# Loading q and k by head pairs, moving casts and rotations between engines, and a reordered front, in an attention-then-MLP kernel

## The chip, the cores and the metric

The kernel runs on one core of one Trainium2 chip. The core has five engines that this text names: TensorE (PE; its weight loads are listed as PEld), VectorE (DVE), ScalarE (ACT), GpSimd (POOL) and SyncE (SP), which here only issues transfers. Sixteen DMA engines move data between DRAM and the on-chip memory SBUF; matrix products land in PSUM. The metric is the device time of one execution in microseconds (us).

## The reference

Banded attention over 8 batches, 8 heads, 576 positions and head width 64, and then a two-layer MLP with an ELU between:

```
scores = q @ k^T / 8                     # per batch and head
scores masked where |row - column| > 32
attn   = exp(scores) / sum(exp(scores))
x      = attn @ v                        # as 4608 tokens x 512
h      = x @ w_in                        # 512 -> 2048
g      = h where h > 0, else exp(h) - 1
out    = g @ w_out                       # 2048 -> 512, float32
```

## The kernel before

**The loop.** The MLP is a loop of 144 steps (`for kk`, L529). A tile of tokens has 256 rows, so there are 18 tiles, and each takes eight steps of two 128-wide groups of the hidden layer. In step kk, TensorE computes `mm1(kk)` (L481, 8 products of 256 columns, L489); ACT takes exp of it (`e_sb`, L495); DVE subtracts 1 (`m_sb`, L497) and, in the next step, takes the ELU (`g_sb`, L502). `mm2` (L508, 4 products of 512 columns, L516) lags two steps behind. At a tile's last step its result is copied out of PSUM by ACT and DVE and written by a transfer of SP (L524 to L526). Up to step 18 `mm1` has two buffers in PSUM, after that three.

**The attention.** Queries are taken in 36 pairs of 64-row blocks, each block against the 128 keys around it. A pair is spread over three steps: `scores` (L277, 32 small products for a pair of blocks counted with both heads of a head pair; then exp on ACT into `pu`, L291), `mask` (DVE, L300), `pv` (L304, products with v and a column of ones, L312), `normalize` (DVE, L321 and L324, into `x_st`), and a transpose of `x_st` into `xT`: by TensorE and a DVE copy for pairs 0 to 7 (`x_transpose` L329, `x_evac` L345), by a transposing transfer on SP's queue from pair 8 on (`x_dma`, L348). Tile t of the MLP needs pairs 2t and 2t+1. Pair i of 8 and more begins at step max(4(i-2)-6, begin of the pair before + 3).

**q and k.** They arrive in float32 (`load_qk`, L107, tile `f`) with 96 partitions, each holding 6 positions of all 8 heads: for one transfer both sides count 96 outermost, then 8 heads, then a run of 768 or 1536 bytes. They are needed transposed, the head width on the partitions, as `qT` and `kT`. For batch 0 they come in halves and are cast to bfloat16 by DVE and ACT (`cast_qk`, L215), transposed on TensorE (`transpose_qk`, L257, 96x96 each, tile `ptx`, L265) and copied out of PSUM. Batch 1 likewise, in halves, at steps 7 to 17. For batches 2 to 4 the casts run on POOL (L463), two to three steps ahead of the transposes (L464), with the copies on ACT. For batches 5 to 7 ACT casts them (`cast_rows`, L236), a transfer on ACT's queue writes them to DRAM (`write_rows`, L247), and a transposing transfer on SP's queue reads them back (`transpose_rows`, L253).

**v and the weights.** They are cast while they are transferred, by POOL's queue (`load_v` L119, `load_w_in` L140, `load_w_out` L147). v lies in `V_e`; a copy moved by 64 rows, `V_o`, is made by two transfers of SP (`rotate_v`, L127). Each weight comes in four chunks; chunk c is needed from step 0, 2, 8 and 12 on.

**What sets the order.** All of it is written out by hand: each engine runs its instructions in the order in which the program emits them, and `at(step, slot, function)` (L404) places attention work in the slots of a step ("dve" after the ELU, "mid" after `mm1`, "end" after `mm2`). An instruction that waits holds up everything behind it on its engine or queue. A `gate` (L135) is a one-element transfer on SP's queue that waits for a weight chunk, and so holds back the loads behind it. Tiles are reused in rings: two buffers each for `f`, three for V.

Of the kernel before, what the change touches and what calls it, by code (L numbers as in the profile page):

```python
# [15 lines left out]
def _bap(ap, new_ap, off=0):  # L16
    return bass.AP(tensor=ap.tensor, offset=ap.offset + off,
                   ap=[list(x) for x in new_ap])
# [3 lines left out]
def kernel(  # L22
# [19 lines left out]
    NQB = S // QB  # L42
    NPAIR = B * NQB // 2
    HP = H // 2
    SJ = 6
    SP_ = S // SJ
    VS = 5
    VD = D + 1

# [36 lines left out]
    def ps_tile(shape, dt, tag, name):  # L86
        return pools[tag].tile(shape, dt, tag=tag, name=name)
# [18 lines left out]

    def load_qk(b, which, part):  # L107
        z, nj = part
        if (b, which) not in qk_f:
            qk_f[b, which] = lpool.tile([SP_, H * SJ * D], FP32,  # L110
                                        tag=f"f{which}", name=f"f{which}")
        t = qk_f[b, which]
        n = H * nj * D
        nc.sync.dma_start(
            out=t[:, z * n:(z + 1) * n].rearrange("p (h x) -> p h x", h=H),
            in_=(q, k)[which][b, :, z * SP_ * nj:(z + 1) * SP_ * nj, :]
            .rearrange("h (p j) d -> p h (j d)", j=nj))

    def load_v(b, m):  # L119
        lo = 128 * m - WIN  # L120
# [5 lines left out]

    def rotate_v(b, m0=0, m1=VS - 1):  # L127
        e, o = V_e[b % 3], V_o[b % 3]
        nc.sync.dma_start(out=o[0:64, m0:m1], in_=e[64:128, m0:m1])
        nc.sync.dma_start(out=o[64:128, m0:m1], in_=e[0:64, m0 + 1:m1 + 1])  # L130

    gate_t = cpool.tile([1, 8], BF16, name="gate_t")
    gates = [0]
# [20 lines left out]
    def w_in_at(c):  # L154
        return w_in_sb[0:1, 0, (c + 1) * (D_FF // 4) - 1:(c + 1) * (D_FF // 4)]

    for i in range(3):
        nc.vector.memset(V_e[i][:, :, :, D:VD], 1.0)
        nc.vector.memset(V_e[i][0:32, 0], 0.0)
        nc.vector.memset(V_e[i][96:128, VS - 1], 0.0)  # L160
        if i < 2:
            for c0, n in ((KPAD - WIN, HP), (KPAD + HP * S, 1)):
                z = kT[i][:, c0:c0 + WIN]
                nc.vector.memset(_bap(z, [z.ap[0], [S, n], [1, WIN]]), 0.0)
# [4 lines left out]
    for part in (HALF_A, HALF_B):  # L169
        for which in range(2):  # L170
            load_qk(0, which, part)
    for m in (1, 2, 0, 3, 4):
        load_v(0, m)
    rotate_v(0, 0, 2)
    rotate_v(0, 2, VS - 1)
    load_w_in(0)


# [30 lines left out]
    def copy_on(eng, d_, s_):  # L209
        if eng is nc.scalar:  # L210
            nc.scalar.copy(d_, s_)  # L211
        else:
            eng.tensor_copy(d_, s_)  # L213

    def cast_qk(b, which, part, hps, eng):  # L215
        z, nj = part
        hp0, nh = hps[0], 2 * len(hps)
        n = H * nj * D
        s_ = qk_f[b, which][:, z * n + 2 * hp0 * nj * D:
                            z * n + (2 * hp0 + nh) * nj * D]  # L220
        s_ = _bap(s_, [s_.ap[0], [nj * D, nh], [D, nj], [1, D]])
        t = lpool.tile([SP_, nj, nh * D], BF16, tag=f"b{which}", name="qkb",
                       bufs=4)
        qk_b[b, which, z, hp0] = t
        copy_on(eng, _bap(t, [t.ap[0], [D, nh], [nh * D, nj], [1, D]]), s_)

    def keys_or_queries(b, which):
        if which == 0:
            return qT[b % 2]
        return kT[b % 2][:, KPAD:KPAD + HP * S].rearrange(  # L230
            "p (g s) -> p g s", g=HP)


    rows, in_dram = {}, {}

    def cast_rows(b, which, hp):  # L236
        if hp == 0:
            rows[b, which] = lpool.tile([SP_, SJ, H * D], BF16,
                                        tag=f"r{which}", name="rows", bufs=1)
        n = SJ * D  # L240
        s_ = qk_f[b, which][:, 2 * hp * n:(2 * hp + 2) * n]
        d_ = rows[b, which][:, :, 2 * hp * D:(2 * hp + 2) * D]
        nc.scalar.copy(  # L243
            _bap(d_, [d_.ap[0], [D, 2], [H * D, SJ], [1, D]]),
            _bap(s_, [s_.ap[0], [n, 2], [D, SJ], [1, D]]))

    def write_rows(b, which):  # L247
        t = dpool.tile([S, H * D], BF16, tag=f"d{which}", name="in_dram")
        in_dram[b, which] = t
        nc.scalar.dma_start(  # L250
            out=t.rearrange("(p j) c -> p j c", j=SJ), in_=rows.pop((b, which)))

    def transpose_rows(b, which):  # L253
        nc.sync.dma_start_transpose(
            out=keys_or_queries(b, which), in_=in_dram.pop((b, which)))

    def transpose_qk(b, which, part, hps, evac, tag="t0"):  # L257
        z, nj = part
        src = qk_b.pop((b, which, z, hps[0]))
        nh = len(hps)  # L260
        W = 512 if nh > 1 else 1024
        pt = ps_tile([128, nh, W], BF16, tag, "ptx")
        for g in range(nh):
            for j in range(nj):
                nc.tensor.transpose(  # L265
                    pt[:, g, j * SP_:(j + 1) * SP_],
                    src[:, j, g * 128:(g + 1) * 128], ident[0:SP_, 0:SP_])
        n = SP_ * nj
        d = keys_or_queries(b, which)[:, hps[0]:hps[0] + nh, z * n:(z + 1) * n]
        pitch = d.ap[1][0] if nh > 1 else n  # L270
        copy_on(evac,
                _bap(d, [d.ap[0], [pitch, nh], [nj, SP_], [1, nj]]),
                _bap(pt, [pt.ap[0], [W, nh], [1, SP_], [SP_, nj]]))

    st = {}

# [65 lines left out]
            xT[t] = xpool.tile([128, 2, NDO, 128], BF16, tag="xT", name="xT")  # L342
        return xT[t][:, z, :, :]

    def x_evac(i):  # L345
        nc.vector.tensor_copy(xT_of(i), st.pop(i))  # L346

    def x_dma(i):  # L348
        x_st = st.pop(i)[3]
# [4 lines left out]
        return NQB * b // 2  # L354


    warm = cpool.tile([128, 1], FP32)
    nc.vector.memset(warm, 0.0)
    nc.scalar.activation(warm, warm, AX.Exp)

    def front_qk(part, tags):
        for g in range(2):
            hps = (2 * g, 2 * g + 1)
            cast_qk(0, 0, part, hps, nc.vector)
            cast_qk(0, 1, part, hps, nc.scalar)
            transpose_qk(0, 0, part, hps, nc.scalar, tags[g])
            transpose_qk(0, 1, part, hps, nc.vector, tags[2 + g])

    front_qk(HALF_A, ("h0", "h1", "y0", "y1"))
    for i, tag in ((0, "s"), (1, "u")):  # L370
        scores(i, tag)
    for i in (0, 1):
        mask(i)
    front_qk(HALF_B, ("h0", "h1", "y0", "y1"))
    for fn in (pv, normalize, x_transpose, x_evac):
        for i in (0, 1):
            fn(i)

    gate(w_out_sb[0:1, NFO // 4 - 1, D_MODEL - 1:D_MODEL])
    for which in range(2):  # L380
# [3 lines left out]
    for c in range(2, 4):  # L384
        load_w_in(c)
        load_w_out(c)
    rotate_v(1, 0, 2)
    gate(w_in_at(3))
    for which in range(2):
        load_qk(1, which, HALF_B)  # L390
    for m in range(3, VS):
        load_v(1, m)
    rotate_v(1, 2, VS - 1)
    for which in range(2):
        load_qk(2, which, WHOLE)
    for m in range(VS):
# [7 lines left out]
    def at(kk, slot, fn, *args):  # L404
        tasks.setdefault((kk, slot), []).append((fn, args))
# [14 lines left out]
    for i, tag in ((2, "s"), (3, "u")):  # L420
        at(0, "mid", scores, i, tag)
        at(1, "dve", mask, i)
        at(1, "mid", pv, i)
        at(2, "dve", normalize, i)
        at(2, "mid", x_transpose, i)
        at(3, "dve", x_evac, i)
    at(4, "dve", swap_pools)

    allh = tuple(range(HP))
    for part, kq in ((HALF_A, 8), (HALF_B, 16)):  # L430
        for which in range(2):
            at(kq - 1, "mid", cast_qk, 1, which, part, allh,
               (nc.scalar, nc.vector)[which])
            at(kq + which, "mid", transpose_qk, 1, which, part, allh,
               nc.scalar, "s")
    pair_at(4, 10)
    pair_at(5, 13)
    pair_at(6, 18)
    pair_at(7, 21)

# [2 lines left out]
    for i in range(8, NPAIR):  # L443
        kk = begin[i] = max(HALF * (i - 2) - 6, begin[i - 1] + 3)
        at(kk, "mid", scores, i)
        at(kk + 1, "dve", mask, i)
        at(kk + 1, "end", pv, i)
        at(kk + 2, "dve", normalize, i)
        at(kk + 2, "end", x_dma, i)
    for b in range(2, B):  # L450
        k0 = begin[first_pair(b)]
        if b >= 3:
            kk = max(k0 - 26 if b < 5 else k0 - 36, 18)
            at(kk, "mid", load_qk, b, 0, WHOLE)
            at(kk + 1, "mid", load_qk, b, 1, WHOLE)
            for m in range(VS):
                at(kk + 2 + m // 3, "mid", load_v, b, m)
        if b < 5:
            for n in range(2 * HP):
                which, hp = n // HP, n % HP  # L460
                kk = k0 - (8 if b == 2 else 10) + n
                at(kk - 2 - b // 3, "mid", cast_qk, b, which, WHOLE, (hp,),
                   nc.gpsimd)  # L463
                at(kk, "mid", transpose_qk, b, which, WHOLE, (hp,), nc.scalar)  # L464
        else:
            for which in range(2):
                c0 = k0 - 27 + 8 * which
                for hp in range(HP):
                    at(c0 + (0, 1, 4, 5)[hp], "end", cast_rows, b, which, hp)
                at(c0 + 6, "mid", write_rows, b, which)  # L470
                at(c0 + 9, "mid", transpose_rows, b, which)
        at(k0 - HALF, "mid", rotate_v, b)

# [94 lines left out]
```

The softmax here doesn't subtract the row's maximum and nothing guards it: scores larger than these inputs give would overflow.

## Time and profile before

The median of 13 runs is 337.62 us (335.95 to 343.52). The profiled execution took 337.12 us in all, of which its span, first instruction to last, is 335.3; 1.8 us lie around it. Its granted TensorE clock was 0.998.

| | |
|---|---|
| first `mm1` begins | 26.46 us |
| step 16, 32, 48, 97, 143 begins | 64.34, 104.75, 140.82, 239.21, 326.56 us |
| last product ends, span ends | 330.5, 335.3 us |
| q and k of batch 0, second half of k landed | 14.91 us |
| first chunk of w_in, second of w_out landed | 19.84, 30.46 us |
| ACT, cast of 96x768 (`rows`) | 820 ns |
| ACT, copy of 128x512 (`y_sb`); exp 128x1024 (`pu`) | 587, 1018 ns |
| ACT, copy of a transposed 128x576, 128x1152 | 633, 1118 ns |
| DVE, cast of 96x1536; copy of 128x512 bfloat16 out of PSUM | 944, 415 ns |
| DVE, ELU; minus 1 (medians) | 692, 427 ns |

Steps are counted in the timeline by the groups of eight products of L489. In the profile's rows, "out<-in" names the tiles, xN the count, "<-" after a bracket what ended the idle time before an instruction; a queue's engine is written with a q (SPq). The windows view gives, for each stretch, its length and then each engine's busy time with the number of its instructions.

### The profile page before, as it was taken

The page shows a single profiled execution, that of the slowest core. Times are in us where ns is not written, and L with a number is a line of the kernel's source. Part 1 is how long each engine was busy: PE and PEld are TensorE (multiplying, and loading weights), DVE is VectorE, ACT ScalarE, POOL GpSimd, SP SyncE. Part 2 cuts the span into 40 slices and gives each one's busy share as a digit, 9 for nine tenths or more (in the row PEclk, how much of TensorE's full clock was granted, in tenths as well). Part 3 has the DMA queues.
Part 4 walks back from the last instruction along what each step waited for, and adds up shares of the span by engine and source line. Part 5 has one row for each costly group of instructions (what it writes and reads, how often), then busy time and mean ns, then how long its engine had stood idle before and what let it go on. Part 6 is the DMA issues. An engine that isn't in the chain of part 4 may idle for free.

```text
span 335.3 us, 7736 instructions
## 1 busy us (share of the span) xinstructions
PE 303.3 (90%) x3152; PEld 201.5 (60%) x3152; DVE 240.3 (72%) x446; ACT 171.5 (51%) x262; POOL 63.4 (19%) x84
## 2 busy tenths in 40 slices
PE   0347999798899998899999999999999999999994
PEld 0235666565666665576666666666666666666661
DVE  4456767687686779676778777687878777877662
ACT  1624265565556634488655566566644443443431
POOL 8442320086461119100111100000000000000000
PEclk9999999999999999999999999999999999999999
DMA  8999999999999999948999999979492320202011
GB/s 174 186 229 206 212 182 190 216 287 228 127 154 170 231 203 185 165 91 168 184 233 221 172 259 199 229 138 251 83 158 74 86 80 18 78 18 81 0 63 63
DMA packets 93862, 52.72 MB, mean 157 GB/s; under 512 B 67908, under 2 KB 87364, under 8 KB 93828
## 3 DMA queue, kind: packets, MB, share of 16 engines
q1 hardware_dynamic: 51428, 39.79, 56.4%
q0 software_dynamic: 41728, 8.92, 39.2%
q10 hardware_dynamic: 672, 3.54, 3.3%
q8 instruction: 24, 0.39, 0.5%
q14 instruction: 10, 0.08, 0.1%
HBM read 36.70 MB, written 12.98 MB: 148 GB/s over the span
## 4 chain that ended last, share of the span: by engine, by line
PE 80%; DMA 7%; DVE 6%; ACT 3%; issue 2%; SPq 0%; DVEq 0%
PE ps L489 36%; PE psY L516 34%; DMA xT<-x_st 4%; PE psS L312 3%; PE psS L284 3%; PE ptx L265 3%; DMA f<-in_k_dram 2%; DMA Vo<-Ve 2%; DVE m_sb L497 1%; DVE g_sb L502 1%; ACT e_sb L495 1%; DVE x_st L324 1%; ACT pu L291 1%; ACT qkb L211 1%; DVE xT L346 1%
## 5 line engine op out<-in xcount | busy, mean ns | idle before, releaser
L495 ACT ACTIVATE e_sb<-ps 128x512 f32<-128x512 f32 x144 | 86.0, 597 | 144.1 <-PE ps L489 142.0
L489 PE MATMUL ps<-xT,w_in_sb 128*128 128x256 bf16 x1152 | 150.8, 274 | 5.1 <-DVE xT L346 3.3
L516 PE MATMUL psY<-w_out_sb,g_sb 128*128 128x512 bf16 x576 | 148.1, 379 | 0.3 <-DVE g_sb L502 0.2
L489 PEld LDWEIGHTS <-w_in_sb 128*128 128x128 bf16 x1152 | 110.4, 98 | 42.4 <-issue 5.0
L502 DVE SCALAR_TENSOR_TENSOR g_sb<-ps,m_sb 128x512 bf16<-128x512 f32 x144 | 99.4, 690 | 13.8 <-DVE m_sb L497 0.5
L497 DVE TENSOR_SCALAR m_sb<-e_sb 128x512 bf16<-128x512 f32 x144 | 67.4, 468 | 57.9 <-ACT e_sb L495 56.4
L516 PEld LDWEIGHTS <-g_sb 128*128 128x128 bf16 x576 | 52.6, 98 | 38.6 <-DVE g_sb L502 0.7
L123 POOL DMA_DIRECT2D Ve<-in_v_dram x40 | 34.1, 858 | 95.7 <-PE psS L312 81.3
L291 ACT ACTIVATE pu<-psS 128x1024 bf16<-128x1024 f32 x36 | 36.5, 1019 | 1.8 <-PE psS L284 1.6
L265 PE MATMUL ptx<-ident,qkb 96*128 96x96 bf16 x240 | 17.6, 221 | 14.8 <-DVE qkb L213 12.3
L324 DVE TENSOR_TENSOR x_st<-psS,rc 128x512 bf16<-128x512 f32 x36 | 24.9, 692 | 3.4 <-DMA xT<-x_st 2.3
L300 DVE TENSOR_TENSOR pm<-pu,masks 128x1024 bf16<-128x1024 bf16 x36 | 25.2, 701 | 2.2 <-ACT pu L291 2.0
L213 POOL CAST qkb<-f 96x768 bf16<-96x768 f32 x24 | 20.8, 904 | 29.3 <-DMA f<-in_q_dram 23.6
L265 PEld LDWEIGHTS <-qkb 96*128 96x128 bf16 x240 | 14.3, 105 | 16.7 <-DVE qkb L213 12.9
L312 PEld LDWEIGHTS <-pm 128*64 128x64 bf16 x576 | 12.5, 113 | 17.3 <-DVE pm L300 12.0
L243 ACT CAST rows<-f 96x768 bf16<-96x768 f32 x24 | 19.7, 822 | 0.0
L312 PE MATMUL psS<-Ve,pm 128*64 128x65 bf16 x320 | 16.5, 200 | 0.5 <-DVE pm L300 0.3
L284 PE MATMUL psS<-qT,kT 64*128 64x64 bf16 x576 | 15.3, 196 | 1.6 <-DVE xT L346 0.9
L312 PE MATMUL psS<-Vo,pm 128*64 128x65 bf16 x256 | 14.5, 200 | 2.4 <-DMA Vo<-Ve 1.6
L284 PEld LDWEIGHTS <-kT 64*128 64x128 bf16 x576 | 11.2, 98 | 9.0 <-issue 7.6
L211 ACT COPY qT<-ptx 128x576 bf16<-128x576 bf16 (+1 forms) x18 | 12.4, 689 | 4.4 <-PE ptx L265 4.4
L525 DVE COPY y_sb<-psY 128x512 f32<-128x512 f32 x18 | 12.3, 685 | 2.0 <-PE psY L516 2.0
(29 smaller groups left out, 64.6 us busy)
## 6 DMA issues: line engine op xcount, KB each, us to landing
out_dram<-y_sb SPq DMA_DIRECT2D x18, 512.0 KB, 3.3
f<-in_q_dram SPq DMA_DIRECT2D x6, 1152.0 KB, 12.4
f<-in_k_dram SPq DMA_DIRECT2D x6, 1152.0 KB, 15.3
in_dram<-rows ACTq DMA_DIRECT2D x6, 576.0 KB, 3.8
Vo<-Ve SPq DMA_DIRECT2D x12, 260.0 KB, 5.0
Ve<-in_v_dram POOLq DMA_DIRECT2D x24, 128.0 KB, 13.1
f<-in_q_dram SPq DMA_DIRECT2D x4, 576.0 KB, 9.7
f<-in_k_dram SPq DMA_DIRECT2D x4, 576.0 KB, 12.0
```

The lines of the kernel that those rows point to most:

```text
L123: nc.gpsimd.dma_start(out=V_e[b % 3][p0:p1, m, :, 0:D], in_=v[b, :, lo + p0:lo + p1, :].rearrange("h p d -> p h d"))
L265: nc.tensor.transpose(pt[:, g, j * SP_:(j + 1) * SP_], src[:, j, g * 128:(g + 1) * 128], ident[0:SP_, 0:SP_])
L284: nc.tensor.matmul(psS[:, h % 2, hp * 128 + z * QB:hp * 128 + (z + 1) * QB], lhsT=kT[b % 2][base:base + 64, KPAD + hp * S + QB * qb - WIN: ...
L291: nc.scalar.activation(pu, _bap(psS, [psS.ap[0], [1, 1024]]), AX.Exp, scale=SCALE)
L300: nc.vector.tensor_mul(pm, pu, _bap(mm, [mm.ap[0], [0, H], [1, 2 * QB]]))
L312: nc.tensor.matmul(psS[QB * z:QB * (z + 1), par, hp * VD:(hp + 1) * VD], lhsT=pm[:, par * HP + hp, z * QB:(z + 1) * QB], rhs=vv[:, qb // 2 ...
L324: nc.vector.tensor_mul(x_st, _bap(psS, [psS.ap[0], [VD, HP], [512, 2], [1, D]]), _bap(rc, [rc.ap[0], [2, HP], [1, 2], [0, D]]))
L489: nc.tensor.matmul(ps[:, j, :], lhsT=w_in_sb[:, do, fo * 128:(fo + 1) * 128], rhs=xT[t][:, :, do, :], start=(do == 0), stop=(do == NDO - 1))
L495: nc.scalar.activation(e_sb, ps, AX.Exp)
L497: nc.vector.tensor_scalar(m_sb, e_sb, -1.0, None, ALU.add)
L502: nc.vector.scalar_tensor_tensor(g_sb, psH.pop(kk), 0.0, m_t.pop(kk), ALU.max, ALU.min)
L516: nc.tensor.matmul(psY[t][ts], lhsT=g_sb[:, j, ts * 128:(ts + 1) * 128], rhs=w_out_sb[:, s * FG + j, :], start=(s == 0 and j == 0), stop=( ...
```

## The change

- q and k are loaded with 128 partitions: a partition holds 18 positions (9 in the halves) of two heads, four head pairs by 32 runs of positions. Each load is two transfers, one for each head of the pairs. The source of a transfer counts 4 outermost, then 32, then a run of 2304 or 4608 bytes; the destination counts 128, then that run.
- Casts go by positions, 768 columns each for whole batches, and all are on ACT or DVE, none on POOL. Transposes on TensorE are 128x128: 18 for each of q and k of a batch, where it was 24 of 96x96.
- Batches 3 to 7 go through DRAM (before: 5 to 7). Batch 2 is cast by ACT from step 17 on and transposed on TensorE in steps 19 to 26. Batches 3 to 7 are loaded 30 steps ahead of their first pair (batch 3 at step 18) and cast from 18 steps ahead on.
- `rotate_v` is two DVE copies of 64 partitions, 2080 columns for a whole batch, where it was two transfers.
- In the front, casts and transposes are regrouped (q, then k, each in pieces of 5 and 4 positions), copies of `xT` go to ACT, and `idle(n)` puts n products of zeros, 512 columns each, into TensorE's order at six places.
- Pairs 4 and 5 begin one step earlier (9 and 12).

```diff
     def load_qk(b, which, part):
         z, nj = part
-        n = H * nj * D
-        nc.sync.dma_start(
-            out=t[:, z * n:(z + 1) * n].rearrange("p (h x) -> p h x", h=H),
-            in_=(q, k)[which][b, :, z * SP_ * nj:(z + 1) * SP_ * nj, :]
-            .rearrange("h (p j) d -> p h (j d)", j=nj))
+        t = lpool.tile([128, 2, nj * D], FP32, tag=f"f{which}{nj}",
+                       name=f"f{which}")
+        qk_f[b, which, z] = t
+        src = (q, k)[which][b, :, z * NC * nj:(z + 1) * NC * nj, :].rearrange(
+            "(g h) (c j) d -> g c h (j d)", h=2, j=nj)
+        for h in range(2):
+            nc.sync.dma_start(out=t[:, h, :], in_=src[:, :, h, :])
...
     def rotate_v(b, m0=0, m1=VS - 1):
         e, o = V_e[b % 3], V_o[b % 3]
-        nc.sync.dma_start(out=o[0:64, m0:m1], in_=e[64:128, m0:m1])
-        nc.sync.dma_start(out=o[64:128, m0:m1], in_=e[0:64, m0 + 1:m1 + 1])
+        nc.vector.tensor_copy(o[0:64, m0:m1], e[64:128, m0:m1])
+        nc.vector.tensor_copy(o[64:128, m0:m1], e[0:64, m0 + 1:m1 + 1])
...
+    def idle(n, tag):
+        ps = ps_tile([128, 512], FP32, tag, "ps_idle")
+        for _ in range(n):
+            nc.tensor.matmul(ps, lhsT=zeros[:, 0:128], rhs=zeros,
+                             start=True, stop=True)
...
+    idle(12, "y1")
+    front_cast(0, HALF_A, nc.vector)
+    front_transpose(0, HALF_A, nc.scalar, ("h0", "h1"))
+    idle(5, "u")
+    front_cast(1, HALF_A, nc.scalar)
+    front_transpose(1, HALF_A, nc.vector, ("y0", "y1"))
     for i, tag in ((0, "s"), (1, "u")):
         scores(i, tag)
+    idle(8, "h1")
+    front_cast(0, HALF_B, nc.vector)
+    front_transpose(0, HALF_B, nc.scalar, ("h0", "h1"))
     for i in (0, 1):
         mask(i)
-    front_qk(HALF_B, ("h0", "h1", "y0", "y1"))
-    for fn in (pv, normalize, x_transpose, x_evac):
-        for i in (0, 1):
-            fn(i)
+    front_cast(1, HALF_B, nc.scalar)
+    idle(4, "y1")
+    front_transpose(1, HALF_B, nc.scalar, ("y0", "y1"))
+    rotate_v(0, 0, 2)
+    idle(4, "h1")
+    for i in (0, 1):
+        pv(i)
+    for i in (0, 1):
+        normalize(i)
+    rotate_v(0, 2, VS - 1)
+    idle(4, "h1")
+    for i in (0, 1):
+        x_transpose(i)
+    for i in (0, 1):
+        x_evac(i, nc.scalar)
...
-    pair_at(4, 10)
-    pair_at(5, 13)
+    at(10, "dve", rotate_v, 1, 0, 2)
+    at(17, "dve", rotate_v, 1, 2, VS - 1)
+    pair_at(4, 9)
+    pair_at(5, 12)
...
+    starts = set(begin.values()) | {9, 12, 18}
+    LEAD = 18
     for b in range(2, B):
         k0 = begin[first_pair(b)]
         if b >= 3:
-            kk = max(k0 - 26 if b < 5 else k0 - 36, 18)
+            kk = max(k0 - 30, 18)
             at(kk, "mid", load_qk, b, 0, WHOLE)
             at(kk + 1, "mid", load_qk, b, 1, WHOLE)
...
+        groups = [(which, j0) for which in range(2) for j0 in (0, 6, 12)]
+        if b == 2:
+            free = [f for f in range(17, k0) if f not in starts]
+            for n, (which, j0) in enumerate(groups):
+                at(free[max(n - 1, 0)], "end", cast_qk, b, which, WHOLE, j0,
+                   6, nc.scalar)
+                at(free[n + 1], "mid", transpose_qk, b, which, WHOLE, j0,
+                   6, nc.scalar)
         else:
-            for which in range(2):
-                c0 = k0 - 27 + 8 * which
-                for hp in range(HP):
-                    at(c0 + (0, 1, 4, 5)[hp], "end", cast_rows, b, which, hp)
-                at(c0 + 6, "mid", write_rows, b, which)
-                at(c0 + 9, "mid", transpose_rows, b, which)
-        at(k0 - HALF, "mid", rotate_v, b)
+            free = [f for f in range(k0 - LEAD, k0) if f not in starts]
+            for n, (which, j0) in enumerate(groups):
+                at(free[n], "end", cast_qk, b, which, WHOLE, j0, 6, nc.scalar)
+                if j0 == 12:
+                    at(free[n], "end", write_rows, b, which)
+                    at(free[n] + 4, "mid", transpose_rows, b, which)
+        at(k0 - HALF - 1, "dve", rotate_v, b)
```

The first pair of batches 2 to 7 begins at step 27, 39, 58, 74, 94 and 110 in both kernels.

## The prediction

> **What bounds the kernel now.** I read the page's shares and rows over time first, then the windows by stage, the timeline at the start of the loop, the queues' table, the waits, and last the loads' tile `f`.
>
> ```profile
> PE 303.3 (90%) x3152; PEld 201.5 (60%) x3152; DVE 240.3 (72%) x446; ACT 171.5 (51%) x262; POOL 63.4 (19%) x84
> ...
> PE   0347999798899998899999999999999999999994
> ...
> DMA  8999999999999999948999999979492320202011
> ...
> q1 hardware_dynamic: 51428, 39.79, 56.4%
> ...
> q10 hardware_dynamic: 672, 3.54, 3.3%
> ...
> f<-in_q_dram SPq DMA_DIRECT2D x6, 1152.0 KB, 12.4
> f<-in_k_dram SPq DMA_DIRECT2D x6, 1152.0 KB, 15.3
> ```
>
> TensorE is full but for the first tenth; the DMA engines are full for two thirds of the span. The windows (length, then PE, PEld, DVE, ACT, POOL with counts, clock, DMA share, GB/s):
>
> ```profile
> 0.00:27.00 27.00, 8.93 (x123) 6.88 (x124) 12.72 (x30) 8.88 (x12) 15.14 (x28) 1.00 1.41 198
> ...
> 50.00:130.00 80.00, 74.65 (x873) 50.05 (x871) 60.23 (x106) 44.35 (x69) 30.08 (x36) 1.00 1.40 198
> 130.00:235.00 105.00, 103.21 (x1079) 68.01 (x1077) 79.58 (x149) 65.04 (x101) 11.58 (x14) 1.00 1.15 193
> ```
>
> To 27 us TensorE waits for q and k; then it is the bound. The loop, 26.46 to 330.5, is 304.0 us. A plain step takes 1.735 us (steps 133 and 134 begin at 309.20 and 310.94): 144 x 1.735 = 249.8. Steps 100 to 104, with one pair of attention, take 7.88 us against 4 x 1.735 = 6.94, so a pair costs 0.94: 34 pairs in the loop, 32.0. Transposes of q and k: 24 groups of six at 0.26 and 4 of twelve at 0.51, 8.2; of x, 1.3. That makes 291.3. The other 12.7 us are waits (9.1 from step 3 on, the largest 2.02 at 64.34 and 1.1 at 86.53 and 140.82) and a slow start:
>
> ```profile
> 26.46 1.87 PE L489 MATMUL ps<-xT,w_in_sb 128*128 128x256 bf16 x8 [0.52 <-DVE xT L346]
> ...
> 29.23 1.41 PE L489 MATMUL ps<-xT,w_in_sb 128*128 128x256 bf16 x8
> ```
>
> The same eight products take 0.87 later on.
>
> **The loads, the part that decides.** Now `f`'s source counts 96 outermost, and so does its destination. After the change the source counts 4 outermost (head pairs), then 32, and the destination 128. How many of the 16 DMA engines a transfer uses follows its shape: queue 1's packet records hold 2018 completion packets of 4 bytes, which are 16 for each of the 58 plain transfers (their outermost counts are 64, 96 or 128), 32 for each of the 34 transposing ones, and 1 for each of the two gates, which move one element. Both plain cases fit the largest number up to 16 that divides the outermost counts of both sides. For 4 and 128 that is four engines. No transfer of this trace has such a shape; its ends are sixteen, as for all loads so far, and one, as for a gate. I leave out one, since 4 and 128 share more than a gate's count of 1 does, and take four.
>
> The Trainium skill ("DMA: Bandwidth & Descriptors", sections "Why a DMA increments its semaphore by 16 and not by 1" and "Rules for kernel authors") states the same rule and warns that an outermost count under 16 confines the whole transfer to that many engines; no run here shows a count of 4. By that page the sum is the four-engine one below; by the row of the other loads, the sixteen-engine one.
>
> With four engines: q and k are 16 tensors of 1.18 MB, 18.87 MB, so 4.72 MB for each engine. What one engine moves in 1 us: 13.4 KB in the loads of now (1536 bytes in 115 ns), 14.8 in V_o's copies (4160 bytes in 281 ns), 20.1 in queue 10's writes (6144 bytes in 305 ns mean), 26.3 by their median of 234. The new runs are 2304 and 4608 bytes, and only four engines pull at memory, so I take 17.5, between the middle two: 270 us; the ends are 352 and 180. The same four engines carry their part of everything else. By packet records, on each engine: v 37 us (36,864 packets of 16 ns over 16), weights 20, outputs 16, transposing reads 34, row writes 13; together 120, of which I count three quarters, since beside the loads v's packets, the largest term, cost 12 ns and not 16: 90. Add 2 to begin and 12 for gaps (a load of step kk can't be issued before that step, and a tile of `f` must be free). So k of batch 7 has landed at 374. ACT waits for it in the cast, in step 96 or 97; what is left of the program behind that point takes as long as now, from 239.2 to 335.3, 96. Span 470, with 1.8 around it **472**. Ends: 2 + 352 + 90 + 12 + 96 + 2 = 554, and 2 + 180 + 90 + 12 + 96 + 2 = 382.
>
> This can't be hidden, since ACT runs in order. Now the wait for a load falls on an engine that nothing needs at that time:
>
> ```profile
> POOL qkb L213 <- DMA f<-in_q_dram: 23.6, 2, 21.1
> ```
>
> After, casts stand on ACT behind `mm2`'s slot, with the exp of the next step behind them, so `m_sb`, `g_sb` and `mm2` stop too. SP's queue also holds `x_dma` and the output writes behind the loads. In the front a half is 147 KB for each of four engines, 8.4 us; four of them and v bring k's second half at about 40 and the first `mm1` to about 47. That is part of the chain of loads, so I don't add it.
>
> **The other parts, with sixteen engines.** Against 337.1, the profiled execution (0.5 under the median):
> - Front. Halves of k land at 14.91 now, and with longer runs at about 14.4. From there: two casts on ACT 1.3 (0.82 for 768 columns, so 0.72 and 0.60 for 640 and 512), transposes and zeros to 17.6, pv 0.4, two normalizations 1.8, transposes of x 0.25, ACT's copy 0.6, and 0.3 between engines: first `mm1` at 20.9, 5.5 earlier. If zeros do nothing for the slow start, that is all; if they make the first three steps like the fourth, 0.8 more. Their own cost is nothing while TensorE waits for `f` there; uncovered, 37 products at 0.215 (four products of `mm2`, as long, take 0.86) are 7.9. Bounds: 1.6 lost (6.3 less 7.9) to 6.5 gained; I take 6.3, as the idle first slices speak for cover.
> - Transposes. Batches 3 and 4 leave TensorE: 16 groups at 0.26, 4.2 gained. 18 transposes of 128 columns cost what 24 of 96 do, 2304 columns. The two batches' row writes land 3.8 us after issue and their transposing reads are issued four steps (6.9 us) later, some six steps before the first pair: hidden, and counted in the DMA sum.
> - Waits. Gone: 2.02 at 64.34, 0.47, and 2.2 between 128 and 141, as pair 5 comes a step earlier and POOL's casts go. New: scores of pair 4 at step 9 wait for ACT's copy of kT, 1.4; in steps 16 to 26 ACT has 27.0 us of work (11 exps at 0.6, three `pu` at 1.02, casts and copies of batch 2 and the rest) against 25.3 of TensorE, 2.5; `x_dma` of pair 9 stands behind q and k of batch 4 on SP's queue, where now an `x_dma` behind a load lands 9 to 14 us after issue against 2.4 alone, 4.5 at step 32. With y_sb's 1.0 and the small ones that stay, from 9.1 to 11.3, 2.2 lost. Bounds: 4.7 gained, if nothing new waits, and 8 lost, if the three new ones, 8.4 together, last some 1.7 times as long.
> - `rotate_v` on DVE: two copies of 2080 columns. DVE's cast of 1536 columns took 944 ns, 0.61 a column, so 2 x 1.28 stand ahead of `m_sb` and `g_sb`. DVE is 72% busy and `g_sb` leads `mm2` by little; each pair of copies may hold TensorE by 0.6, six times: 3.6. Bound below 0, if that lead covers it; above, 6 x 2.56 = 15.
>
> The Trainium skill ("VectorE: DVE Perf Modes", perf-mode tiers) has bfloat16 copies within SBUF four elements a cycle; its 693 ns for 2048 elements would leave 1.4 for a pair of copies and no wait. No row here shows such a copy, and by it the sum is the lower one of the next line.
>
> 337.1 - 6.3 - 4.2 + 2.2 = 328.8, and with 3.6 for the rotation 332.4.
>
> **Rivals.**
> 1. *Sixteen engines, the gain arrives*: 329 to 332, **331**; with the bounds 322 to 336. For it: each load of this trace used 16 and its destination still counts 128. Against: the gates.
> 2. *Four engines, but fast*: each engine at 26.3 KB/us because four don't crowd memory: **382**. For it: queue 10's median. Against: 1536 and 768 bytes (13.4 and 13.2) gain nothing by length.
> 3. *Sixteen engines, ACT in the way*: the casts that POOL did (24 at 0.83) are ACT's, and the waits at steps 9 to 32 reach their upper bound: 337.1 - 6.3 - 4.2 + 8 + 3.6, **338**. It decides where these waits and the rotation cost over 10.5 together.
> 4. *The zeros do nothing*: rival 1 with 0.8 less, 332.
>
> **Numbers.** Four engines 0.75: 0.23 near the fast end (under 420), 0.40 in the middle, 0.12 over 520. Sixteen 0.25: faster 0.20, within 0.3% 0.02, slower 0.03 (0.3% is about what a measurement here can tell from no change). Faster 0.20, same 0.02, slower 0.78. The forecast is the likeliest case, 472; its own range is 382 to 554. The two cases stand far apart, so 8 in 10 takes both in: 326 to 545.
>
> **What would show it.** Four engines: the DMA share falls toward a quarter and GB/s under 100 while `f` takes 15 us and more (now 12.4 and 15.3 at six whole loads); the first `mm1` at 40 or later; ACT's waits headed by a cast for `f` with tens of us, TensorE idle before `mm1` or `mm2` in each batch. Sixteen: `f` under 12 us, first `mm1` near 21, POOL without casts, TensorE over 90% busy, and `m_sb` delayed where `rotate_v` stands. The prediction is wrong if the transfer is spread by destination or by single runs. It is wrong in size alone if a whole q or k, 0.295 MB for each of four engines, takes far from 17 us with nothing beside it.

## The result, and the profile after

The changed kernel takes 478.88 us (median of 11 runs, 474.49 to 483.68); the kernel before took 337.09 over 48 runs. The ratio is 1.418, 95% interval 1.415 to 1.422: slower by 142 us, and 7 us from the forecast of 472. The profiled execution has a span of 475.8. Medians here and below are over all runs of a kernel; the ratios and their intervals leave out executions that the chip ran in a slower state, so a ratio can differ from that of the medians.

The page of the changed kernel, in the order of the lines shown of before (busy time, slices of TensorE, its granted clock, DMA share, queue 1, loads):

```profile
PE 333.2 (70%) x3057; PEld 209.0 (44%) x3057; DVE 242.7 (51%) x460; ACT 174.9 (37%) x262; POOL 42.6 (9%) x60
...
PE   3346858666519500599971799508997799999995
...
PEclk8677979977959955699986799776999799999999
DMA  9959969745428969356997889955895671202311
...
q1 hardware_dynamic: 48772, 37.89, 50.5%
...
f<-in_q_dram SPq DMA_DIRECT2D x12, 576.0 KB
f<-in_k_dram SPq DMA_DIRECT2D x12, 576.0 KB
```

TensorE now has holes up to four fifths of the span, and is full only in the last fifth, where no q and k are loaded any more. The clock row has 5 and 6 around the deepest holes. The packet records hold 1666 completion packets on queue 1: 16 for each of 18 output writes, 32 for each of 38 transposing transfers, 1 for each gate, and for the 40 loads 160, which is **4 each**. The same records show how many packets of loads are under way at once: four for 71% of the time in which there are any, and five or more for 2%.

The windows, cut at the first `mm1` and at steps 16, 24, 32, 56 and 97 (length, then PE, PEld, DVE, ACT, POOL, clock, DMA share, GB/s):

```profile
0.00:44.26 44.26, 20.32 (x145) 9.81 (x146) 11.66 (x30) 11.05 (x16) 14.67 (x27) 0.73 1.07 127
44.26:89.00 44.74, 35.07 (x346) 23.26 (x346) 25.07 (x48) 17.74 (x26) 11.66 (x14) 0.92 1.04 115
89.00:141.45 52.45, 25.09 (x212) 15.41 (x210) 17.80 (x33) 18.80 (x27) 2.63 (x3) 0.77 0.41 113
141.45:195.25 53.80, 18.89 (x204) 11.97 (x204) 13.67 (x26) 12.77 (x19) 2.44 (x3) 0.69 1.18 121
195.25:264.43 69.18, 52.24 (x513) 32.85 (x514) 40.24 (x76) 26.64 (x40) 6.97 (x8) 0.87 1.06 110
264.43:379.33 114.90, 90.17 (x813) 56.21 (x814) 64.42 (x121) 47.08 (x72) 4.18 (x5) 0.87 1.20 135
379.33:475.80 96.47, 91.38 (x829) 59.51 (x827) 69.82 (x129) 40.85 (x65) 0.00 (x0) 1.00 0.26 71
```

| stretch | before, us | after, us | lost |
|---|---|---|---|
| to the first `mm1` | 26.5 | 44.3 | 17.8 |
| steps 0 to 15 | 37.9 | 44.7 | 6.9 |
| steps 16 to 23 | 22.2 | 52.5 | 30.3 |
| steps 24 to 31 | 18.2 | 53.8 | 35.6 |
| steps 32 to 55 | 53.9 | 69.2 | 15.3 |
| steps 56 to 96 | 80.6 | 114.9 | 34.3 |
| step 97 to the end | 96.1 | 96.5 | 0.4 |

All 140.5 us of span are lost by step 97, and nearly half of it (65.9) in the sixteen steps from 16 to 31. Who waits there is in the waits (us in total, times, longest) and in SP's own timeline (start, length of the issue, what is issued):

```profile
PE ps L501 <- DMA xT<-x_st: 52.6, 3, 34.2
...
PE psS L265 <- DMA kT<-in_dram: 19.3, 2, 13.0
ACT qkb L209 <- DMA f<-in_q_dram: 19.0, 2, 12.3
...
ACT qkb L209 <- DMA f<-in_k_dram: 16.2, 4, 5.4
```

```profile
152.29 1.19 SPq L115 DMA_DIRECT2D f<-in_q_dram  x2
156.74 17.77 SPq L240 DMA_TRANSPOSE qT<-in_dram  x1
174.55 1.50 SPq L115 DMA_DIRECT2D f<-in_k_dram  x2
176.10 14.45 SPq L331 DMA_TRANSPOSE xT<-x_st  x2
```

The largest stop, 34.2 us before step 32, is `mm1` waiting for `x_dma` of pair 9. On SP's queue it stands behind q of batch 4, a transposing read whose issue held SP for 17.8 us, and k of batch 4. The casts' own waits for `f`, 19.0 and 16.2 on ACT, are smaller. (`psS`, with `kT<-in_dram`, are scores that wait for a transposing read of k.)

### The profile page after: what moved, and what is told of

Its sections match the earlier page's. It is cut to its first block, busy times and chain, and to the rows that moved or that the text cites. A ratio compares the mean times of both kernels' runs of the same rounds, so it can differ in the third digit from the quotient of the medians.

```text
span 475.8 us, 7540 instructions
## 1 busy us (share of the span) xinstructions
PE 333.2 (70%) x3057; PEld 209.0 (44%) x3057; DVE 242.7 (51%) x460; ACT 174.9 (37%) x262; POOL 42.6 (9%) x60
## 4 chain that ended last, share of the span: by engine, by line
PE 42%; DMA 40%; SPq 10%; DVE 3%; issue 2%; POOL 1%; ACT 1%; DVEq 0%; ACTq 0%
PE ps L501 19%; PE psY L528 19%; DMA f<-in_k_dram 11%; DMA xT<-x_st 10%; DMA w_out_sb<-in_moe_w_out_dram 7%; DMA w_in_sb<-in_moe_w_in_dram 6%; DMA kT<-in_dram 6%; SPq L240 4%; SPq L115 3%; SPq L538 2%; PE psS L293 2%; PE psS L265 2%; POOL Ve L121 1%; DVE g_sb L514 1%; DVE m_sb L509 1%
## 5 line engine op out<-in xcount | busy, mean ns | idle before, releaser
L501 PE MATMUL ps<-xT,w_in_sb 128*128 128x256 bf16 x1152 | 160.5, 286 | 77.3 <-DMA xT<-x_st 52.6
L501 PEld LDWEIGHTS <-w_in_sb 128*128 128x128 bf16 x1152 | 114.7, 102 | 120.9 <-DMA xT<-x_st 39.7
L528 PE MATMUL psY<-w_out_sb,g_sb 128*128 128x512 bf16 x576 | 158.5, 400 | 1.2 <-DVE g_sb L514 0.9
L509 DVE TENSOR_SCALAR m_sb<-e_sb 128x512 bf16<-128x512 f32 x144 | 62.6, 435 | 122.4 <-ACT e_sb L507 120.5
L528 PEld LDWEIGHTS <-g_sb 128*128 128x128 bf16 x576 | 55.7, 102 | 45.2 <-issue 8.1
L209 ACT CAST qkb<-f 128x768 bf16<-128x768 f32 (+3 forms) x42 | 34.5, 830 | 35.2 <-DMA f<-in_q_dram 19.0
L265 PE MATMUL psS<-qT,kT 64*128 64x64 bf16 x576 | 15.4, 197 | 24.8 <-DMA kT<-in_dram 19.3
L248 PE MATMUL ptx<-ident,qkb 128*128 128x128 bf16 x108 | 11.2, 263 | 24.5 <-ACT qkb L209 14.7
L265 PEld LDWEIGHTS <-kT 64*128 64x128 bf16 x576 | 11.3, 98 | 32.4 <-DMA kT<-in_dram 19.7
L248 PEld LDWEIGHTS <-qkb 128*128 128x128 bf16 x108 | 8.9, 119 | 28.1 <-ACT qkb L209 16.6
L211 DVE CAST qkb<-f 128x640 bf16<-128x640 f32 (+2 forms) x6 | 3.2, 557 | 24.5 <-DMA f<-in_q_dram 12.6
L352 PE MATMUL ps_idle<-zeros 128*128 128x512 bf16 x37 | 14.2, 546 | 1.3 <-DVE zeros L156 1.3
```

The costliest lines, as they stand in the source:

```text
L265: nc.tensor.matmul(psS[:, h % 2, hp * 128 + z * QB:hp * 128 + (z + 1) * QB], lhsT=kT[b % 2][base:base + 64, KPAD + hp * S + QB * qb - WIN: ...
L501: nc.tensor.matmul(ps[:, j, :], lhsT=w_in_sb[:, do, fo * 128:(fo + 1) * 128], rhs=xT[t][:, :, do, :], start=(do == 0), stop=(do == NDO - 1))
L509: nc.vector.tensor_scalar(m_sb, e_sb, -1.0, None, ALU.add)
L528: nc.tensor.matmul(psY[t][ts], lhsT=g_sb[:, j, ts * 128:(ts + 1) * 128], rhs=w_out_sb[:, s * FG + j, :], start=(s == 0 and j == 0), stop=( ...
```

## The experiments

**Is it the number of engines?** Four kernels, run beside each other. *Pairs apart* gives every load an outermost count of 32 on both sides:

```diff
-        for h in range(2):
-            nc.sync.dma_start(out=t[:, h, :], in_=src[:, :, h, :])
+        for g in range(HP):
+            nc.sync.dma_start(out=t[g * NC:(g + 1) * NC], in_=src[g])
```

> The changed kernel with one edit: each q or k load is four transfers, one for each head pair, with both heads in it, so that the outermost count of source and destination is 32 and not 4 (source) and 128 (destination). Runs of 2304 and 4608 bytes, tiles, casts and everything else stay. Theory (the loads use four engines, and that is the whole loss): f's transfers leave 16 completion packets each, first mm1 at about 21 us, time 331 us (328 to 336). Rival A (casts on ACT, rotations on DVE, or the long runs are the loss): still above 440. Rival B (sixteen engines, but ACT's casts and the copies eat the gain): about 338, first mm1 near 21 all the same.

Measured: 360.4 us, ratio to before 1.062 (1.056 to 1.068). The packet records have 16 completions for each load. Of the 142 us, 118 are gone; rival A is out. But 22 us are left over the kernel before, so neither 331 nor 338 came true, and the first `mm1` begins at 27.2, not at 21.

*92 and 4* puts four engines into the kernel before, by splitting the 96 partitions (`SP_`) of each load; *80 and 16* is its control, with `((0, 80), (80, SP_))`:

```diff
...
+        for p0, p1 in ((0, 92), (92, SP_)):
+            nc.sync.dma_start(out=dst[p0:p1], in_=src[p0:p1])
```

> The kernel before with one edit: each q or k load is two transfers, of 92 and of 4 partitions, so that the outermost counts are 92 and 4, whose largest divisor up to 16 is 4. Nothing else of the change is in it. Theory (four engines alone make the loss, without the new casts, copies and front): 4 completion packets for each such transfer, and a time of about 480 (430 to 560); an engine moves 4.72 MB in 225 us at the 21.8 KB per us that the changed kernel showed for 4608 bytes, in 352 at the 13.4 that 1536 bytes had before. Rival (the loss needs the changed layout): 337, within 4.

> The control of the run with 92 and 4: the kernel before with each q or k load in two transfers, of 80 and of 16 partitions, both divisible by 16. Theory: 16 completion packets each, 337 us (335 to 341). Rival (two transfers where there was one cost much by themselves, by issue or by order on the queue): over 345.

Measured: 489.7 (one run) for 92 and 4, with 4 completions for each such transfer, and 349.6, ratio 1.032 (1.027 to 1.038), for 80 and 16, with 16. So the same loss arises in the kernel before, without any new cast, copy or front. The control costs 12 us, where the theory had none: its rival was right that splitting loads has a price. The waits of the run with 92 and 4 show that POOL and ACT wait for `f`:

```profile
POOL qkb L214 <- DMA f<-in_q_dram: 68.4, 2, 52.8
DVE x_st L325 <- DMA xT<-x_st: 48.6, 4, 17.5
ACT qkb L212 <- DMA f<-in_k_dram: 48.0, 2, 27.7
```

*Two engines* varies the amount, two engines where the changed kernel has four:

```diff
+        for g in (0, 2):
+            for h in range(2):
+                nc.sync.dma_start(out=t[g * NC:(g + 2) * NC, h, :],
+                                  in_=src[g:g + 2, :, h, :])
```

> The dose: the changed kernel with each load in four transfers, for two of the four head pairs and one head each, so that the source counts 2 outermost, then 32. Theory: 2 completion packets each and two engines, q and k's packets take twice as long on them, 9.44 MB at 21.8 KB per us, 433 us instead of 217: time about 700 (620 to 800). Rival (the number of engines isn't set by the outermost count, or the loss isn't in the loads' engines): at most 490.

Measured: 654.6 (one run), with 2 completions for each load. The order sixteen, four, two engines gives 345 to 360 (pairs apart, and the run that follows), 479 and 655: the mechanism is shown from both sides. The packet records agree: two packets of loads are under way at once for 84% of the time with two engines, and some packet of a load is under way for 448 us, against 251 in the changed kernel and 77 with runs outermost, the next run, where sixteen at once is the commonest number. The page of the Trainium skill on DMA ("DMA: Bandwidth & Descriptors", section "Why a DMA increments its semaphore by 16 and not by 1") gives the number of engines as the largest up to 16 that divides both sides' outermost counts; that is borne out here for counts of 4, 92 and 2.

**What is the rest of the change worth, with sixteen engines?** *Runs outermost* keeps two transfers for each load, but the 32 runs of positions stand outermost and the head pairs inside, with the copies and row writes adapted:

```diff
-            "(g h) (c j) d -> g c h (j d)", h=2, j=nj)
+            "(g h) (c j) d -> c g h (j d)", h=2, j=nj)
```

> The changed kernel with its loads left at two transfers each (one for each head of the pairs), but the 32 runs of positions outermost and the 4 head pairs inside them: partition 4c + g where it was 32g + c. The copies out of PSUM and the row writes are adapted; bytes, runs, tiles and instruction counts are the changed kernel's. Theory (four engines are the loss, and splitting loads into more transfers cost the run with pairs apart some 12 to 25 us, as 80 and 16 partitions cost the kernel before 12): 16 completion packets each, 343 us (335 to 352), with a wait of 4 to 16 us left at step 32 where x_dma of pair 9 stands behind the loads of batch 4. Rival A (the forecast's sum with sixteen engines): 331 (328 to 336). Rival B (the number of transfers costs nothing, the other parts of the change lose it): 357 to 363, as with pairs apart.

Measured: 344.8, ratio 1.0166 (1.0115 to 1.0217), and 16 completions for each load. The four engines thus cost 134 of the 142 us, and the rest of the change loses 7. The kernel *without zeros* lets `idle` return at once:

> The run with the 32 runs outermost, without the products of zeros (idle does nothing; no part of the result goes with them). Theory of the forecast: the zeros save the slow clock of the first three steps, 0.8 us, so this is 0.8 slower, within 2 of that run; step 0 begins at the same time or earlier, and the first eight-product groups take 1.9, 1.4 and 1.05 us again. Rival (the zeros stand in the way of transposes in the front): 1 to 4 faster.

Measured: 340.8, ratio 1.0063 (1.0024 to 1.0103): 4 faster than with zeros, not 0.8 slower. The first `mm1` begins at 21.30, and at 23.81 with zeros. One large wait is left in it:

```profile
PE ps L501 <- DMA xT<-x_st: 10.5, 2, 9.9
```

SP's timeline of that kernel shows its cause, the same line-up as in the changed kernel with shorter pieces:

```profile
89.09 1.22 SPq L115 DMA_DIRECT2D f<-in_q_dram  x2
90.80 5.34 SPq L240 DMA_TRANSPOSE qT<-in_dram  x1
96.19 1.24 SPq L115 DMA_DIRECT2D f<-in_k_dram  x2
97.47 3.59 SPq L331 DMA_TRANSPOSE xT<-x_st  x2
```

`x_dma` of pair 9, the first of the two in the last line, is issued at 97.47 only, and step 32, which waits for it, begins at 107.26. *Pairs 8 and 9 on TensorE* takes these pairs from the queue:

```diff
-        at(kk + 2, "end", x_dma, i)
+        if i < 10:
+            at(kk + 2, "end", x_transpose, i)
+            at(kk + 3, "dve", x_evac, i)
+        else:
+            at(kk + 2, "end", x_dma, i)
```

> The run without zeros (32 runs outermost, 340.8), and pairs 8 and 9 are transposed by TensorE and copied by DVE as pairs 4 to 7 are, not by x_dma. Theory (with sixteen engines the forecast's gains are there, and one wait of 9.9 us at step 32 for x_dma of pair 9, queued on SP behind a load and a transposing read, eats them; two transposes cost 0.7): 332 (329 to 335), faster than the kernel before by 1 to 2.5%. Rival (the DMA engines are the bound there, and the wait comes back at a later x_dma or a later transposing read): 337 or more.

Measured: 330.6, ratio 0.974 (0.962 to 0.987); step 32 begins at 99.04. The wait did not come back elsewhere: no stop of TensorE after 20 us is longer than 1.3. Since the kernel before spread from 336 to 347 on that chip, the run was made once more:

> The run with pairs 8 and 9 on TensorE once more, unchanged, beside the one with zeros, and beside the kernel before on another chip, whose runs there were 336 to 347: 330.5 (328 to 333); ratio 0.980 (0.972 to 0.988). Rival (the kernel before was slow on that chip, and the two are closer): 0.99 or more.

Measured: 330.8, ratio 0.975 (0.970 to 0.981). **This version beats both kernels**: 7.6 us under the kernel before on that chip, 148 under the changed one. Its page:

```profile
PE 299.5 (91%) x3028; PEld 197.5 (60%) x3028; DVE 244.6 (75%) x462; ACT 174.6 (53%) x262; POOL 42.8 (13%) x60
...
PE   1377989898999999997999999999999999999993
...
PEclk9999999999999999999999999999999999999998
DMA  8999999994699569999799978960683020202011
```

Between the first two slices and the last TensorE has none under 7, and the clock row has no dip before the last slice.

*Zeros back* puts the products of zeros into that version:

> The run with pairs 8 and 9 on TensorE (330.6), with the products of zeros put back. Theory (as between the two runs with the 32 runs outermost, 344.8 with zeros and 340.8 without: six groups of zeros stand before transposes in TensorE's order, and a lower granted clock in the front comes with them): 2 to 4.5 slower than the same kernel without zeros, beside it on the same chip; first mm1 2 later. Rival (those 4 us came from the wait at step 56, which the zeros only moved; with the queue's wait gone, zeros cost the 1.2 us that were left at step 8): within 1.5.

Measured: 331.7, against 330.8 without, on the same chip. The ratios to the kernel before, 0.982 (0.977 to 0.988) and 0.975 (0.970 to 0.981), lie 2.4 us apart and their intervals overlap, so the runs don't decide between the rival's 1.5 and the theory's 2 to 4.5. The first `mm1` begins at 24.61, 2.5 later; the steps 0 to 2 then take 8.19 us and not 9.38. So zeros do shorten the slow start, by 1.2, and cost twice that ahead of it. The windows of the first 21.7 us, with zeros:

```profile
0.00:21.70 21.70, 16.01 (x131) 7.67 (x133) 9.56 (x24) 9.84 (x14) 15.00 (x27) 0.84 1.24 212
```

and without:

```profile
0.00:21.70 21.70, 7.78 (x108) 5.93 (x109) 12.30 (x30) 10.50 (x16) 14.95 (x27) 1.00 1.24 209
```

TensorE is busy for twice as long, at a granted clock of 0.84 instead of 1.00. In the profiled executions of the two earlier runs step 48 begins at 143.1 both times, with zeros and without, and step 56 at 163.3 and 159.5: most of the 4 us between them belong to a wait at step 56 (4.4 us with zeros, 0.7 without), which does not arise in this version. Why zeros in the front moved it is not settled.

**The rotation.** In the kernel before, alone:

```diff
-        at(k0 - HALF, "mid", rotate_v, b)
+        at(k0 - HALF - 1, "dve", rotate_dve, b)
```

`rotate_dve` holds the change's two `tensor_copy` on DVE.

> The kernel before with one part of the change: rotate_v of batches 2 to 7 is two DVE copies of 64 partitions and 2080 columns, at the dve slot one step ahead of where its two transfers stood. Theory of the forecast (0.61 ns a column, 1.28 us a copy, 0.6 us of TensorE for each of six): 3.6 slower, 341 (338 to 346). Rival A (four elements a cycle, 0.7 us a copy, hidden by the lead of g_sb): 337, within 1.5. Rival B (twelve transfers fewer on SP's queue free x_dma and loads): 332 to 336.

Measured: 340.0, ratio 1.0052 (1.0017 to 1.0088), so 1.8 us slower by the ratio, between the theory and rival A. The tile's line (duration min/median/max in ns) prices the copy:

```profile
L134 DVE COPY Vo<-Ve x6: 697/698/698, 81.7 to 256.4; 64x2080 bf16<-64x2080 bf16 x6
```

0.70 us, not 1.28. The rule of the Trainium skill ("VectorE: DVE Perf Modes", perf-mode tiers; 693 ns for 2048 elements) had the duration right; the forecast took it from a row of a cast from float32, and that was too long. The profiled execution is only 0.4 longer than that of before, so where the 1.8 us arise isn't shown.

*Rotation on POOL* replaces those copies in the version with pairs 8 and 9 on TensorE, one step earlier:

> That run, with rotate_v of batches 2 to 7 on POOL, one step earlier, where DVE had two copies of 0.70 us each. POOL is busy for 13% of the span. Theory (the DVE copies hold up m_sb and g_sb, which cost the kernel before 2.1 us in the run with rotations on DVE): 2 faster than the run with pairs 8 and 9 on TensorE, 0 to 4. Rival (the copies on DVE are hidden, or POOL's are long enough that pv waits for Vo): the same within 1, or slower.

Measured: 334.8, against 330.6 beside it: slower, as the rival has it, though the intervals of the two ratios to the kernel before (0.972 to 1.005 and 0.962 to 0.987) overlap. A copy takes 1.9 to 2.0 us on POOL. The last two end at 199.0, and `pv` of that batch starts at 199.58, but what it waits for is not a copy. It is the mask, which DVE finishes late:

```profile
194.93 2.00 POOL L127 COPY Vo<-Ve 64x2080 bf16<-64x2080 bf16 x1
...
195.86 1.34 DVE L513 TENSOR_SCALAR m_sb<-e_sb 128x512 bf16<-128x512 f32 x1
...
196.98 2.00 POOL L128 COPY Vo<-Ve 64x2080 bf16<-64x2080 bf16 x1
...
197.92 1.60 DVE L281 TENSOR_TENSOR pm<-pu,masks 128x1024 bf16<-128x1024 bf16 x1
...
199.58 0.22 PE L293 MATMUL psS<-Vo,pm 128*64 128x65 bf16 x1 [2.30 <-DVE pm L281]
```

The mask's median is 0.68 us, and that of `m_sb` 0.43. The ten `m_sb` that run beside POOL's twelve copies take 0.83 to 1.67. So moving the copies off DVE lengthened DVE's own work.

**Why did pairs apart cost 16 us more than runs outermost?** *Four transfers* splits the latter's loads into halves of 16 runs, 64 partitions each:

```diff
+        for c in (0, NC // 2):
+            for h in range(2):
+                nc.sync.dma_start(
+                    out=t[c * HP:(c + NC // 2) * HP, h, :],
+                    in_=src[c:c + NC // 2, :, h, :])
```

> The run with the 32 runs outermost (344.8), each load in four transfers and not two: 16 of the 32 runs and one head each, 64 partitions, outermost count 16, so sixteen engines. It has as many transfers as the run with pairs apart (360.4), whose packets of 4608 bytes took 352 ns where they took 222 with the 32 runs outermost. Theory A (the number of transfers costs by issue and order on SP's queue): 357 to 363, packets near 222 ns. Theory B (a transfer that fills only 32 partitions slows its packets, and that is the 16 us): packets between 222 and 300 ns, 345 to 352. Theory C (neither; only transfers into one head pair's 32 partitions are slow): 222 ns and 343 to 347.

Measured: 361.7, ratio 1.069 (1.064 to 1.074), with 4608 bytes in 334 ns. The time is theory A's, the packets are slower than theory B allowed, so none of the three holds as written. What the packet records say together is below, under the hardware. How much of the 17 us is slower packets and how much the number of transfers stays open.

## Why the prediction was right, point by point

- **Four engines.** Right: 4 completions a load, and the kernels that change the outermost counts (pairs apart, 92 and 4, two engines, runs outermost) move as it says; runs outermost keeps the number of transfers too.
- **The sum of 472.** The total is right by errors that cancel, which is luck. The rate of one engine was mis-sized: q and k's packets take 899 us in all, 225 for each of four engines, so 21.0 KB per us and not 17.5, 45 us less than forecast. That counts each packet alone; with other packets between them a whole q or k takes 15.1 to 18.1 us from its first packet to its last, near the 17 that the prediction named as a sign of its size. The other terms were mis-sized the other way: step 97 begins at 379.3, so 154 us lie beside the q and k packets, where 2 + 90 + 12 = 104 were counted. The 12 for gaps was far too small: until the last packet of a load ends, at 362.8, there are 111 us with none under way. The 90 rests on a wrong reading: in the records of the kernel before, v's packets of 128 bytes take 45.6 ns on average and 31 at the least, not 16 (15.7 is the mean of that queue's 4-byte completion packets), so v comes to 105 us for an engine and not 37, and the five terms to some 220 and not 120. What follows step 97 was right: 96.5 for 96.
- **"ACT waits for it in the cast, in step 96 or 97."** This step failed. ACT's last wait for `f` is at 151.2; k of batch 7 is issued at 340, its last packet ends at 362.8, and it is cast at 379 without a wait. The loads are no unbroken chain: each is issued when the program reaches its step, TensorE stops behind the transfers that share the four engines, and this in turn delays the next loads. Of TensorE's eight stops of more than 5 us after the first `mm1`, five, 72 us of 96, are for transposing transfers that stand behind loads. In the waits, 52.6 us are for `x_dma`, whose place behind the loads the prediction named as a side effect of SP's queue, and 19.3 for transposing reads of k, which its sum for sixteen engines took as hidden. One stop of 11.8, at 129.6, comes from ACT's longest wait for `f`. This path is read from the waits; no run with four engines moves the transposing transfers off SP's queue.
- **The front.** Forecast about 47, measured 44.3; k's second half is cast from about 37.
- **The signs.** GB/s fell, to 112 and not under 100. The DMA share did not fall toward a quarter: it stays at 9 in many slices, since packets that share the four engines with the loads take longer in the records, presumably because their times contain waiting. The 256-byte packets of the transposing transfers take 59 ns here on average and 27 with runs outermost. The completions were the better sign.
- **The other parts, with sixteen engines.** 331 was forecast, 344.8 measured with the zeros, over the bounds (336) and over rival 3 (338). The mis-sized terms: `x_dma` of pair 9, which was named at step 32 with 4.5, took 9.8; a wait of 4.4 at step 56 was not foreseen; zeros moved the first `mm1` from 21.3 to 23.8, where 20.9 was forecast. 331 + 5.3 + 4.4 + 2.9 = 343.6. The waits were also added wrongly: 9.1 less 4.7 and plus 8.4 is 12.8, not 11.3. ACT's overload in steps 16 to 26 (2.5) is not to be seen: these steps take 28.1 us, with zeros and without, and 29.1 before. The rotation cost 1.8 in the kernel before, where 3.6 was counted. The version without the queue's wait and the zeros measures 330.6, but this does not confirm the sum of 331: without its 4.5 for `x_dma` and with 0.7 for two more transposes it would be 327, or near 329 with the waits added rightly, so 2 to 3 us stay unexplained.

## What to carry to other kernels

Before a load is laid out anew, write down the outermost count of both of its sides; if one has no divisor near 16, the transfer has fewer engines, and what shares its queue and its engines waits with it, here `x_dma` and the transposing reads. Afterwards, count the completion packets rather than read the DMA share. A small transfer that is due soon doesn't belong behind large loads on the same queue: two pairs moved off it were worth 10 us here, more than the whole front.

## What the runs showed of the hardware

- In these runs packets are faster where a transfer over sixteen engines fills all 128 partitions. 4608 bytes take 222 ns on average with 128 (runs outermost), 334 with 64, 352 with 32; 1536 bytes took 115 with the 96 of the kernel before, which is 345 for 4608. The runs with 64 and 32 also have twice as many transfers, and what that does to a packet is not separated. On four engines (92 and 4 partitions) a packet of 1536 takes 78 ns, so the limit isn't the single engine. The Trainium skill ("SBUF — State Buffer", section "Door 1: The DMA port swizzle (why [64,N] ≈ [32,N])") says that partitions 0 to 63 reach only the eight ports that 0 to 31 reach. The near agreement of 334 and 352 fits that; why 96 is no faster it doesn't say, and no run here shows the ports.
- A wait costs more than its length. After 34.2 us without work the next eight products take 1.89 us, where 1.04 is usual in this view (the 0.87 of the prediction is from the chain that ended last, where a piece ends as the next begins), and the stretches with most waiting have granted clocks of 0.69 and 0.77 against 1.00 at the end:

```profile
195.25 1.89 PE L501 MATMUL ps<-xT,w_in_sb 128*128 128x256 bf16 x8 [34.19 <-DMA xT<-x_st]
```

- Work on POOL can lengthen work on DVE. Beside POOL's copies of V, `m_sb` takes 0.83 to 1.67 us where 0.43 is its median; beside POOL's casts of q and k in the kernel before, up to 1.96. `g_sb` keeps its 0.69 beside both:

```profile
L497 DVE TENSOR_SCALAR m_sb<-e_sb x144: 408/427/1957, 29.0 to 328.3; 128x512 bf16<-128x512 f32 x144
L502 DVE SCALAR_TENSOR_TENSOR g_sb<-ps,m_sb x144: 675/692/694, 29.5 to 328.8; 128x512 bf16<-128x512 f32 x144
```
